# The sums of the output weights' quarters, formed on VectorE behind the first half of the first y instead of on GpSimd

## The chip, the core and the metric

The kernel runs on one core of one Trainium2 chip. Its time is the device time of one execution in microseconds; the time before is 693.48 us, the median of 3 runs (693.12 to 696.33). In the text PE is TensorE's matrix engine, PEld its weight loads, DVE is VectorE, ACT ScalarE, POOL GpSimd, and SP the engine that issues the DMAs.

## The reference, cut to what matters

The program is a chain of three stages on a batch of 4 with 576 positions and 512 channels: an attention (a pooled one and a local one, added), a mixer with two pairs of weights, and a last mixer with cosines and sines. Only the last is touched by the change:

```python
theta = x @ w_theta
zr, zi = x * np.cos(theta), x * np.sin(theta)
y = einsum('ts,bsd->btd', w_tok_r, zr) + einsum('ts,bsd->btd', w_tok_i, zi)
u = x + y
out = u + np.maximum(u @ w_ch, 0.0)
```

All of it is float32 and has to stay so. Each operand of a product is therefore split in two parts that TensorE takes at full rate, a high part and the rest (names that end in h and l), and each product is three matmuls: high by high, high by low, low by high (`mm3`, lines 137 to 139). `split` (lines 132 and 133) makes the parts: a cast on ACT and a subtraction on DVE.

## The kernel before, in words

Attention and the first mixer are issued in an order written out by hand, a table at the head of the kernel. The last mixer, which comes after that table, is written as a loop over the four batches `b`; there the framework's scheduler decides by a timeline of its own in which order the instructions stand on each engine. Within one engine the order is then fixed, and each engine works through its queue in that order, waiting on semaphores of the others.

Per batch the last mixer has four steps.
- `stage_z`: the product th of the transposed x (`xh`, `xl`) with `w_theta`, in blocks of 128 positions. Each block is evicted by ACT (`tt`, line 843), its angle reduced on DVE (`tf`, lines 844 and 847), cosine and sine taken on ACT (`tg` and `tf`, lines 849 to 851), multiplied by x on DVE (line 855; line 863 for the last 64 positions, which two batches share in tiles `eh`, `el`), and split into `zh` and `zl` (lines 132 and 133). For batch 0 it is called twice, for columns 0 to 255 and 256 to 511, with names th_0_... and th_256_...; for the others once.
- `stage_y`: y in four quarters of channels, each in two halves of 288 positions. A quarter's half is 27 matmuls of 288 columns (9 blocks of `z` by three). `stage_y(b, 0, ...)` makes the first two quarters (four results, 108 matmuls), `stage_y(b, 1, ...)` the other two (108 more). Line 879 adds each result to x in place, on DVE.
- sums of u for a scheme with seven products instead of eight (`first_sum`, `other_sums`, `split_sums`, with the tile `us`, which shares a buffer by the tag raw).
- `stage_out`: the seven products of `u` with `w_ch` (banks named o_a to o_d), combined and stored.

The seven products also need sums of the quarters of `w_ch`, once for all batches. That is `weight_sums`: `wc_whole` is the whole of the weights, high plus low, 2048 columns a partition; four sums of 512 columns follow (`wc_sums`), three of which are split into `sums` and `suml` and one into a quarter of `wch` and `wcl`. It is called in batch 0 behind the first `stage_y`, and is done on POOL, except for the two splits. `wc_whole` has no buffer of its own: it takes the one of the tag x in `cells["cx"][1]` that `load_x(1)` will fill with the x of batch 1 (tile cx, a DMA of 1152 KB, line 733). So that load waits for the last reader of `wc_whole`. `load_x(b)` also loads x in the other orientation (cxn, line 739). The x of batch 1 is split into `cxh` and `cxl` (line 1015 of the kernel before, 1017 of the changed one), which th of batch 1 needs.

Of the kernel before, what the change touches and what calls it, by code (L numbers as in the profile page):

```python
# [12 lines left out]
F32 = mybir.dt.float32  # L13
# [6 lines left out]
ALU = mybir.AluOpType  # L20
# [67 lines left out]
HALF = S // 2  # L88
# [10 lines left out]
def kernel(  # L99
# [16 lines left out]
    act, dve, pool, pe, sp = nc.scalar, nc.vector, nc.gpsimd, nc.tensor, nc.sync  # L116
# [14 lines left out]
    def split(hi, lo, src):  # L131
        act.copy(hi, src)  # L132
        dve.tensor_tensor(out=lo, in0=src, in1=hi.bitcast(F32), op=ALU.subtract)  # L133

    def mm3(out, lh, ll, rh, rl, start, stop, again=False):

        pe.matmul(out, lh, rh, start=start, stop=False, skip_group_check=again)  # L137
        pe.matmul(out, lh, rl, start=False, stop=False, skip_group_check=again)  # L138
        pe.matmul(out, ll, rh, start=False, stop=stop, skip_group_check=again)  # L139
# [589 lines left out]
    def load_x(b):  # L729

        x = cells["cx"][b % 2].tile([128, 4, S if b % 2 else 640], F32, tag="x", name=f"cx_{b}")
        src = xT_d.rearrange("(k p) n -> p k n", p=128)
        sp.dma_start(x[:, :, 0:S], src[:, :, b * S : b * S + S])
        if b % 2 == 0:

            sp.dma_start(x[:, :, S:640], src[:, :, b * S + S + 512 : b * S + 2 * S])
        xn = cells["cx"][0].tile([128, NB, DM], F32, tag="xn", name=f"cxn_{b}", bufs=1)
        rows = xN_d[b * S : b * S + S]
        sp.dma_start(xn[:, 0:4], rows[0:512].rearrange("(k p) d -> p k d", p=128))
        if b % 2 == 0:  # L740
            for j in range(2):
                sp.dma_start(xn[64 * j : 64 * j + 64, 4], xN_d[(b + j) * S + 512 : (b + j) * S + S])
        return x, xn

    def split_x(b, x):
        xh = cells["cs"].tile([128, 4, 640], F32R, tag="xh", name=f"cxh_{b}")
        xl = cells["cs"].tile([128, 4, 640], F32R, tag="xl", name=f"cxl_{b}")
        n = 512 if b % 2 else 640
        steps = []
        for kb in range(4):  # L750
            h, l, r = xh[:, kb, 0:n], xl[:, kb, 0:n], x[:, kb, 0:n]
            steps.append(partial(act.copy, h, r))
            steps.append(partial(dve.tensor_tensor, out=l, in0=r, in1=h.bitcast(F32), op=ALU.subtract))
        return (xh, xl), steps
# [55 lines left out]
    op = ctx.enter_context(tc.tile_pool(name="op", bufs=2))  # L810
    turns = count()

    def bank(name):
        return psum(next(turns), name)

    cells["cx"].append(ctx.enter_context(tc.tile_pool(name="cx1", bufs=1, side="right")))
    thh, thl, wrh, wrl, wch, wcl = (cells[name] for name in ("thh", "thl", "wrh", "wrl", "wch", "wcl"))
# [3 lines left out]
    def new_z(b):  # L821
        z = tuple(sb1.tile([128, 8, DM], F32R, tag=f"z{p}", name=f"z{p}_{b}") for p in "hl")
        for e in range(0 if b % 2 else 2):
            last[b + e] = [sb2.tile([128, DM], F32R, tag=f"e{p}", name=f"e{p}_{b + e}") for p in "hl"]
        return z
# [43 lines left out]
    def stage_y(b, hh, x, uh, ul, zh, zl):  # L869
        for db in range(2):  # L870
            k = 2 * hh + db
            c = slice(k * 128, (k + 1) * 128)
            for th in range(2):
                t = slice(th * HALF, (th + 1) * HALF)
                ps = bank(f"y_{b}_{hh}_{db}_{th}")
                for kb in (8, 0, 1, 4, 5, 2, 3, 6, 7):
                    h, l = (e[:, c] for e in last[b]) if kb == 8 else (zh[:, kb, c], zl[:, kb, c])
                    mm3(ps[:, 0:HALF], h, l, wrh[:, kb, t], wrl[:, kb, t], kb == 8, kb == 7)
                dve.tensor_tensor(out=x[:, k, t], in0=ps[:, 0:HALF], in1=x[:, k, t], op=ALU.add)  # L879
            n = S if hh else HALF  # L880
            split(uh[:, k, 0:n], ul[:, k, 0:n], x[:, k, 0:n])

    T0, T1 = slice(0, HALF), slice(HALF, S)
    sums = sb1.tile([128, 3, 2, 256], F32R, name="sums")
# [2 lines left out]
    def raw_sums(name, shape):  # L887
        both = sb1.tile([128, 4 * 2 * HALF], F32, tag="raw", name=name)
        n = 2 * shape
        return [both[:, i * n : (i + 1) * n].rearrange("p (k n) -> p k n", k=2) for i in range(4)], both  # L890

    def weight_sums():

        w = cells["cx"][1].tile([128, 4, S], F32, tag="x", name="wc_whole")[:, :, 0:DM]
        pool.tensor_tensor(out=w, in0=wch.bitcast(F32), in1=wcl.bitcast(F32), op=ALU.add)
        a11, a12, a21, a22 = w[:, 0:2, 0:256], w[:, 2:4, 0:256], w[:, 0:2, 256:DM], w[:, 2:4, 256:DM]
        (s1, s2, s4, s3), both = raw_sums("wc_sums", 256)
        pool.tensor_tensor(out=s1, in0=a21, in1=a22, op=ALU.add)
        pool.tensor_tensor(out=s2, in0=s1, in1=a11, op=ALU.subtract)
        pool.tensor_tensor(out=s4, in0=a12, in1=s2, op=ALU.subtract)  # L900
        pool.tensor_tensor(out=s3, in0=a11, in1=a21, op=ALU.subtract)
        split(*(t.rearrange("p a k n -> p (a k n)") for t in (sums, suml)), both[:, 0 : 3 * 512])
        split(wch[:, 0:2, 256:DM], wcl[:, 0:2, 256:DM], s3)

    def first_sum(b, x):

        (t1, *rest), both = raw_sums(f"us_{b}", HALF)
        dve.tensor_tensor(out=t1, in0=x[:, 0:2, T1], in1=x[:, 0:2, T0], op=ALU.subtract)
        return t1, *rest, both

    def split_sums(b, raws, i, n):
        if i == 0:
            raws += tuple(
                cells["cs"].tile([128, 4, 2, HALF], F32R, tag=tag, name=f"{tag}s_{b}") for tag in ("xh", "xl")
            )
        both, *hl = raws[4:]
        h, l = (t[:, i : i + n].rearrange("p a k n -> p (a k n)") for t in hl)
        split(h, l, both[:, i * 2 * HALF : (i + n) * 2 * HALF])
        return raws

    def other_sums(b, x, raws):

        t1, t2, t3, t4 = raws[0:4]
        dve.tensor_tensor(out=t2, in0=x[:, 2:4, T1], in1=t1, op=ALU.subtract)
        dve.tensor_tensor(out=t3, in0=x[:, 2:4, T1], in1=x[:, 0:2, T1], op=ALU.subtract)
        dve.tensor_tensor(out=t4, in0=x[:, 2:4, T0], in1=t2, op=ALU.subtract)
# [73 lines left out]
    z = new_z(0)  # L1000
    stage_z(0, 0, 256, *xhl, xx[1], *z)
    stage_z(0, 256, DM, *xhl, xx[1], *z)
    for b in range(B):
        x, xn = xx
        uh = sb1.tile([128, 4, S], F32R, tag="uh", name=f"cuh_{b}")
        ul = sb1.tile([128, 4, S], F32R, tag="ul", name=f"cul_{b}")
        stage_y(b, 0, x, uh, ul, *z)
        if b == 0:
            weight_sums()
        raws = first_sum(b, x)  # L1010
        if b + 1 < B:
            xx = load_x(b + 1)
            xhl, steps = split_x(b + 1, xx[0])
            for st in steps:
                st()
        else:
            raws = split_sums(b, raws, 0, 1)
        stage_y(b, 1, x, uh, ul, *z)
        other_sums(b, x, raws)
        if b + 1 < B:  # L1020
            z = new_z(b + 1)
            stage_z(b + 1, 0, DM, *xhl, xx[1], *z)
            raws = split_sums(b, raws, 0, 1)
        split_sums(b, raws, 1, 1)
        split_sums(b, raws, 2, 2)
        stage_out(b, x, uh, ul, *raws[-2:])
# [70 lines left out]
```

## Time and profile before

| | |
|---|---|
| runs of the kernel | 693.12, 693.48, 696.33 us |
| the profiled execution's own time | 693.91 us |
| its span | 692.1 us |
| PE busy | 666.8 us, 96% of the span |
| DVE, ACT, POOL busy | 474.2, 304.4 and 106.6 us |
| share of the chain that ended last: PE, DVE, DMA, ACT | 85%, 5%, 5%, 2% |

The busy times are a first hint only: an engine can be busy with something that nobody waits for. The chain that ended last is followed back from the end, and says at each step what released the next. [...] A row of a timeline is: start in us, duration in us, engine, line, operation, what it writes and reads, shape, count, and in brackets the idle time before it and who ended that. Starts are counted from the start of the span; the hand-ordered part ends at about 472 us, where the last mixer begins.

### The profile page before, as it was taken

What the parts mean: (1) busy time and instruction counts of PE and PEld (TensorE: products, weight loads), DVE (VectorE), ACT (ScalarE), POOL (GpSimd) and SP (SyncE); (2) the same over time, 40 slices, a digit from 0 to 9 for tenths busy, and PEclk for the clock granted to TensorE, in tenths of its full rate; (3) what the DMA queues carried; (4) which work ended last, traced back from release to release, by engine and by line L of the source; (5) the groups of instructions that cost most, each with busy time, mean ns of one, the idle gap of its engine ahead of it and who ended that gap; (6) DMA issues with size and microseconds to landing.
All of it is one profiled execution on the core that took longest, in us unless ns stands there. A gap on an engine that the chain in (4) does not pass through costs nothing.

```text
span 692.1 us, 17284 instructions
## 1 busy us (share of the span) xinstructions
PE 666.8 (96%) x7368; PEld 637.1 (92%) x7368; DVE 474.2 (69%) x835; ACT 304.4 (44%) x594; POOL 106.6 (15%) x84
## 2 busy tenths in 40 slices
PE   7679899999999999999999999999799999999997
PEld 5558789999999999999999999999798998998997
DVE  6798998764543888997783423446967847857837
ACT  4466667352442565656361212113646326526311
POOL 3143222201000332452421000003200000000000
PEclk9779999999999999999999999999999999999999
DMA  8697787554334776744473483465210420140202
GB/s 286 207 283 230 247 279 252 182 175 137 125 107 158 230 241 212 229 156 141 143 203 75 121 228 95 94 159 114 70 62 1 135 87 0 52 147 1 70 1 69
DMA packets 85613, 100.36 MB, mean 145 GB/s; under 512 B 44257, under 2 KB 65889, under 8 KB 85537
## 3 DMA queue, kind: packets, MB, share of 16 engines
q1 hardware_dynamic: 85536, 99.27, 46.6%
q8 instruction: 58, 0.95, 0.6%
q14 instruction: 19, 0.15, 0.1%
HBM read 74.34 MB, written 24.90 MB: 143 GB/s over the span
## 4 chain that ended last, share of the span: by engine, by line
PE 85%; DVE 5%; DMA 5%; ACT 2%; issue 1%; SPq 1%; DVEq 0%; ACTq 0%
PE c L646 7%; PE c L137 7%; PE c L138 7%; PE c L649 7%; PE c L139 7%; PE c L647 7%; PE y L139 6%; PE y L137 6%; PE y L138 6%; PE t L137 2%; PE th L139 2%; PE th L138 2%; PE th L137 2%; PE t L138 2%; PE t L139 2%; PE o L515 1%
## 5 line engine op out<-in xcount | busy, mean ns | idle before, releaser
L190 POOL TENSOR_TENSOR ww<-ww,raw 128x512 int32<-128x512 int32 (+2 forms) x43 | 65.3, 1524 | 186.0 <-DVE ww L186 89.2
L662 ACT ACTIVATE g<-c 128x384 fp32r<-128x384 f32 x72 | 34.3, 493 | 105.8 <-PE c L139 90.5
L137 PE MATMUL y<-wrh,zh 128*128 128x288 f32 x256 | 75.6, 298 | 3.2 <-ACT zh L132 3.2
L138 PE MATMUL y<-wrl,zh 128*128 128x288 f32 x256 | 75.5, 297 | 0.0
L139 PE MATMUL y<-wrh,zl 128*128 128x288 f32 x256 | 73.5, 297 | 0.4 <-DVE zl L133 0.4
L665 DVE SCALAR_TENSOR_TENSOR g<-c,g 128x384 fp32r<-128x384 f32 x72 | 37.8, 551 | 46.3 <-ACT g L662 39.5
L673 DVE TENSOR_TENSOR ut<-c,ut 128x384 f32<-128x384 f32 x48 | 25.7, 549 | 38.1 <-PE c L649 29.2
L137 PEld LDWEIGHTS y<-wrh,zh 128*128 128x128 f32 x256 | 48.5, 190 | 3.5 <-ACT zh L132 3.5
L138 PEld LDWEIGHTS y<-wrl,zh 128*128 128x128 f32 x256 | 48.5, 189 | 0.0
L139 PEld LDWEIGHTS y<-wrh,zl 128*128 128x128 f32 x256 | 47.6, 189 | 0.8 <-DVE zl L133 0.8
L173 ACT ACTIVATE ww<-raw 128x512 f32<-128x512 f32 (+2 forms) x43 | 29.2, 679 | 24.7 <-DMA raw<-w_ch 10.1
L879 DVE TENSOR_TENSOR cx<-y,cx 128x288 f32<-128x288 f32 x32 | 14.6, 456 | 35.7 <-PE y L139 35.3
L132 ACT CAST cuh<-cx 128x288 fp32r<-128x288 f32 (+1 forms) x16 | 8.9, 554 | 61.6 <-DVE cx L879 61.6
L174 ACT ACTIVATE raw<-raw 128x512 int32<-128x512 uint32 (+3 forms) x48 | 31.9, 665 | 0.0
L139 PE MATMUL th<-thh,cxl 128*128 128x512 f32 (+1 forms) x92 | 31.6, 343 | 0.0
L138 PE MATMUL th<-thl,cxh 128*128 128x512 f32 (+1 forms) x92 | 31.6, 343 | 0.0
L137 PE MATMUL th<-thh,cxh 128*128 128x512 f32 (+1 forms) x92 | 31.6, 343 | 0.0
L186 DVE SCALAR_TENSOR_TENSOR ww<-raw,ww 128x512 uint32<-128x512 uint32 (+2 forms) x43 | 30.4, 707 | 1.5
L176 DVE TENSOR_SCALAR ww<-ww 128x512 f32<-128x512 f32 (+2 forms) x43 | 22.9, 532 | 4.8 <-ACT ww L173 4.5
L178 DVE TENSOR_SCALAR ww<-ww 128x512 uint32<-128x512 uint32 (+2 forms) x43 | 23.1, 537 | 1.5
L843 ACT ACTIVATE tt<-th 128x512 f32<-128x512 f32 (+1 forms) x19 | 10.7, 571 | 25.6 <-PE th L139 24.3
L345 POOL TENSOR_TENSOR vd<-vd 128x650 f32<-128x650 f32 x8 | 11.8, 1478 | 63.5 <-DMA vd<-vtok 63.5
(290 smaller groups left out, 2154.5 us busy)
## 6 DMA issues: line engine op xcount, KB each, us to landing
raw<-w_ch SPq DMA_DIRECT2D x28, 512.0 KB
qk<-qkT SPq DMA_DIRECT2D x16, 582.0 KB
xT<-ut SPq DMA_DIRECT2D x12, 768.0 KB
vd<-vtok SPq DMA_DIRECT2D x8, 650.0 KB
raw<-w_ri SPq DMA_DIRECT2D x9, 576.0 KB
vw<-vloc SPq DMA_DIRECT2D x32, 146.2 KB
uT<-us SPq DMA_DIRECT2D x16, 288.0 KB
ut<-uT SPq DMA_DIRECT2D x6, 768.0 KB
```

The costliest lines, as they stand in the source:

```text
L137: pe.matmul(out, lh, rh, start=start, stop=False, skip_group_check=again)
L138: pe.matmul(out, lh, rl, start=False, stop=False, skip_group_check=again)
L139: pe.matmul(out, ll, rh, start=False, stop=stop, skip_group_check=again)
L173: act.activation(w, high, AF.Abs)
L174: act.activation(f, words[:, :, 0], AF.Copy, scale=2.0**-29)
L186: dve.scalar_tensor_tensor(out=wu, in0=words[:, :, 1], scalar=0xC0000000, in1=wu, op0=ALU.bitwise_and, op1=ALU.bitwise_or)
L190: pool.tensor_tensor(out=w.bitcast(I32), in0=w.bitcast(I32), in1=f, op=ALU.add)
L646: pe.matmul(ps[:, 0:MIX], h[:, cb % 2, d], h1, start=cb == cbs[0], stop=False)
L647: pe.matmul(ps[:, 0:MIX], l[:, cb % 2, d], h1, start=False, stop=False)
L649: pe.matmul(ps[:, 0:MIX], weight[cb // 2][2][:, cb % 2, d], h2, start=False, stop=cb == cbs[-1])
L662: act.activation(h1, ps, AF.Relu)
L665: dve.scalar_tensor_tensor(out=h2, in0=ps, scalar=0.0, in1=h1.bitcast(F32), op0=ALU.max, op1=ALU.subtract)
```

## The change

`weight_sums` uses DVE in place of POOL for its five operations, and is issued only after the last addition of the first `stage_y` (the result y_0_1_1: batch 0, second quarter, second half). For that `stage_y` returns its last addition. Nothing is removed.

```diff
@@ stage_y
                 for kb in (8, 0, 1, 4, 5, 2, 3, 6, 7):
                     h, l = (e[:, c] for e in last[b]) if kb == 8 else (zh[:, kb, c], zl[:, kb, c])
                     mm3(ps[:, 0:HALF], h, l, wrh[:, kb, t], wrl[:, kb, t], kb == 8, kb == 7)
-                dve.tensor_tensor(out=x[:, k, t], in0=ps[:, 0:HALF], in1=x[:, k, t], op=ALU.add)
+                added = dve.tensor_tensor(out=x[:, k, t], in0=ps[:, 0:HALF], in1=x[:, k, t], op=ALU.add)
             n = S if hh else HALF
             split(uh[:, k, 0:n], ul[:, k, 0:n], x[:, k, 0:n])
+        return added
@@ weight_sums
-        pool.tensor_tensor(out=w, in0=wch.bitcast(F32), in1=wcl.bitcast(F32), op=ALU.add)
+        dve.tensor_tensor(out=w, in0=wch.bitcast(F32), in1=wcl.bitcast(F32), op=ALU.add)
...
-        pool.tensor_tensor(out=s1, in0=a21, in1=a22, op=ALU.add)
-        pool.tensor_tensor(out=s2, in0=s1, in1=a11, op=ALU.subtract)
-        pool.tensor_tensor(out=s4, in0=a12, in1=s2, op=ALU.subtract)
-        pool.tensor_tensor(out=s3, in0=a11, in1=a21, op=ALU.subtract)
+        dve.tensor_tensor(out=s1, in0=a21, in1=a22, op=ALU.add)
+        dve.tensor_tensor(out=s2, in0=s1, in1=a11, op=ALU.subtract)
+        dve.tensor_tensor(out=s4, in0=a12, in1=s2, op=ALU.subtract)
+        dve.tensor_tensor(out=s3, in0=a11, in1=a21, op=ALU.subtract)
@@ the loop over batches
-        stage_y(b, 0, x, uh, ul, *z)
+        added = stage_y(b, 0, x, uh, ul, *z)
         if b == 0:
-            weight_sums()
+            with tc.issue_after(added.ins):
+                weight_sums()
```

Up to the first products y the order on every engine is the same as before; behind it the scheduler set the instructions anew. In the lists below a row is: line, operation, what it writes and reads with the numbers of the tiles, shape.

On DVE, at the first split of `z` of batch 0, the difference is this (- is before, + is now):

```order
 L855 TENSOR_TENSOR tg_0_0_6600<-tg_0_0_6600,cxn_5950 128x512
 L855 TENSOR_TENSOR tf_0_0_6599<-tf_0_0_6599,cxn_5950 128x512
-L133 TENSOR_TENSOR wcl<-wc_sums,wch 128x2x256
 L133 TENSOR_TENSOR zl_6538<-tg_0_0_6600,zh_6537 128x2x256
 L855 TENSOR_TENSOR tg_0_2_6640<-tg_0_2_6640,cxn_5950 128x512
```

The split of a sum of weights (`wcl`) stood ahead of the first `zl`, and is gone from there.

Where the five sums now stand on DVE, behind the addition of y_0_1_1 (this is the changed kernel alone; before, the second split `suml` stood some 30 rows earlier, ahead of the third `zl`):

```order
L879 TENSOR_TENSOR cx_5947<-y_0_1_1_6854,cx_5947 128x288
L133 TENSOR_TENSOR zl_6538<-tg_256_2_6750,zh_6537 128x2x256
L896 TENSOR_TENSOR wc_whole<-wch,wcl 128x4x512
L133 TENSOR_TENSOR zl_6538<-tf_256_2_6749,zh_6537 128x2x256
L899 TENSOR_TENSOR wc_sums<-wc_whole 128x512
L902 TENSOR_TENSOR wc_sums<-wc_whole 128x512
L900 TENSOR_TENSOR wc_sums<-wc_sums,wc_whole 128x512
L901 TENSOR_TENSOR wc_sums<-wc_whole,wc_sums 128x512
L133 TENSOR_TENSOR wcl<-wc_sums,wch 128x2x256
L879 TENSOR_TENSOR cx_5947<-y_1_0_0_6912,cx_5947 128x288
L879 TENSOR_TENSOR cx_5947<-y_1_0_1_6941,cx_5947 128x288
L133 TENSOR_TENSOR suml<-wc_sums,sums 128x1536
```

The first sum stands ahead of the last `zl` of batch 0, the other four behind it, and the splits `wcl` and `suml` among the additions of the second `stage_y`.

On PE, behind the last matmul of y of batch 0 (y_1_1_1), where th of batch 1 begins (the names th_0_0 to th_0_3 are its four blocks):

```order
 L139 MATMUL y_1_1_1_7001<-wrh,zl_6538 128x288
+L137 MATMUL th_0_0_7037<-thh,cxh_6902 128x512
 L138 MATMUL th_0_0_7037<-thl,cxh_6902 128x512
+L137 MATMUL th_0_1_7065<-thh,cxh_6902 128x512
+L138 MATMUL th_0_1_7065<-thl,cxh_6902 128x512
+L137 MATMUL th_0_2_7093<-thh,cxh_6902 128x512
+L138 MATMUL th_0_2_7093<-thl,cxh_6902 128x512
+L137 MATMUL th_0_3_7121<-thh,cxh_6902 128x512
+L138 MATMUL th_0_3_7121<-thl,cxh_6902 128x512
+L137 MATMUL o_0_a<-cuh_6763,wch 128x288
+L138 MATMUL o_0_a<-cul_6764,wch 128x288
+L139 MATMUL o_0_a<-cuh_6763,wcl 128x288
```

Before, the first matmuls of th_0_0 stood among those of y, and the four blocks came one after the other; now all of th comes behind all of y, two matmuls of each block first, and four of the first output product among them. On SP the load of cxn for batch 1 now stands ahead of that of cx, and not behind it.

## Rows read from the trace of the kernel before

**Rows 1.** Chain that ended last, where the last mixer begins: start us, us, engine, tile, line.

```profile
474.42 3.12 DVE tf L844
...
491.69 0.61 PE y L139
```

**Rows 2.** Waits of PE, 470 to 692 us: in total, times, longest.

```profile
PE y L137 <- ACT zh L132: 3.2, 1, 3.2
PE y L139 <- DVE zl L133: 0.4, 1, 0.4
```

**Rows 3.** Busy us (and instructions) of PE, PEld, DVE, ACT, POOL; clock, DMA share, GB/s.

```profile
491.00:688.00 197.00, 196.53 (x1353) 189.46 (x1351) 140.79 (x265) 84.39 (x149) 0.00 (x0) 0.99 0.17 58
```

**Rows 4.** Timeline of PE, 486 to 540 us: y, th and first products of batch 1.

```profile
486.76 0.29 PE L137 MATMUL y<-wrh,eh 128*128 128x288 f32 x1
...
490.54 0.51 PE L137 MATMUL y<-wrh,zh 128*128 128x288 f32 x1 [3.22 <-ACT zh L132]
...
503.00 0.30 PE L137 MATMUL y<-wrh,eh 128*128 128x288 f32 x1
...
506.61 0.29 PE L137 MATMUL y<-wrh,eh 128*128 128x288 f32 x1
...
521.90 0.39 PE L138 MATMUL th<-thl,cxh 128*128 128x512 f32 x1
...
522.37 0.39 PE L137 MATMUL th<-thh,cxh 128*128 128x512 f32 x1
...
531.90 0.30 PE L137 MATMUL o_a<-cuh,wch 128*128 128x288 f32 x1
...
535.49 0.29 PE L138 MATMUL o_c<-xls,sums 128*128 128x288 f32 x1
```

**Rows 5.** One-microsecond stretches, columns as in the third group.

```profile
490.00:491.00 1.00, 0.46 (x2) 0.40 (x2) 1.00 (x3) 1.00 (x2) 0.00 (x0) 0.84 0.70 78
...
493.00:494.00 1.00, 1.00 (x6) 1.00 (x5) 0.93 (x3) 1.00 (x2) 0.00 (x0) 0.50 0.98 381
...
494.00:495.00 1.00, 1.00 (x9) 1.00 (x8) 1.00 (x2) 1.00 (x3) 0.00 (x0) 0.96 0.12 42
```

**Rows 6.** Durations by line, DVE, 470 to 692 us: ns shortest/median/longest, first and last start.

```profile
L844 DVE TENSOR_SCALAR tf<-tt x19: 295/423/3105, 474.4 to 643.1; 128x512 f32<-128x512 f32 x17, 128x256 f32<-128x256 f32 x2
...
L847 DVE TENSOR_TENSOR tf<-tt,tf x19: 424/686/1776, 477.6 to 645.5; 128x512 f32<-128x512 f32 x17, 128x256 f32<-128x256 f32 x2
...
L855 DVE TENSOR_TENSOR tg<-tg,cxn x16: 679/686/1751, 488.1 to 649.5; 128x512 f32<-128x512 f32 x16
...
L133 DVE TENSOR_TENSOR xls<-us,xhs x12: 750/754/1356, 533.0 to 680.9; 128x576 fp32r<-128x576 f32 x8, 128x1152 fp32r<-128x1152 f32 x4
...
L133 DVE TENSOR_TENSOR el<-tt,eh x6: 417/556/1515, 481.6 to 588.3; 128x256 fp32r<-128x256 f32 x4, 128x512 fp32r<-128x512 f32 x2
...
L133 DVE TENSOR_TENSOR suml<-wc_sums,sums x1: 1751/1751/1751, 494.2 to 494.2; 128x1536 fp32r<-128x1536 f32 x1
```

**Rows 7.** Timeline of POOL, 360 to 560 us: the first sum, and two of four.

```profile
472.76 4.62 POOL L895 TENSOR_TENSOR wc_whole<-wch,wcl 128x2048 f32<-128x2048 f32 x1 [107.58 <-PE c L649]
...
483.44 1.30 POOL L898 TENSOR_TENSOR wc_sums<-wc_whole 128x512 f32<-128x512 f32 x1 [6.06 <-ACT tg L849]
...
487.69 1.60 POOL L900 TENSOR_TENSOR wc_sums<-wc_whole,wc_sums 128x512 f32<-128x512 f32 x1
```

**Rows 8.** Timeline of ACT, 470 to 565 us.

```profile
474.00 0.39 ACT L843 ACTIVATE tt<-th 128x256 f32<-128x256 f32 x1 [17.52 <-PE th L139]
...
489.87 0.62 ACT L132 CAST zh<-tg 128x512 fp32r<-128x512 f32 x1 [0.54 <-DVE tg L855]
...
526.66 0.60 ACT L843 ACTIVATE tt<-th 128x512 f32<-128x512 f32 x1 [2.12 <-PE th L139]
...
560.07 2.61 ACT L1015 CAST cxh<-cx 128x640 fp32r<-128x640 f32 x4 [4.34 <-DMA cx<-xT]
```

**Rows 9.** Timeline of SP's queue: the loads of x for batches 1 and 2.

```profile
489.31 0.38 SPq L733 DMA_DIRECT2D cx<-xT  x1
...
552.61 0.39 SPq L733 DMA_DIRECT2D cx<-xT  x1
```

**Rows 10.** Timeline of DVE, 470 to 565 us.

```profile
483.84 1.18 DVE L844 TENSOR_SCALAR tf<-tt 128x512 f32<-128x512 f32 x1 [0.30 <-ACT tt L843]
...
486.38 1.78 DVE L847 TENSOR_TENSOR tf<-tt,tf 128x512 f32<-128x512 f32 x1
...
491.56 0.68 DVE L855 TENSOR_TENSOR tg<-tg,cxn 128x512 f32<-128x512 f32 x1
492.16 0.68 DVE L855 TENSOR_TENSOR tf<-tf,cxn 128x512 f32<-128x512 f32 x1
...
533.04 0.75 DVE L133 TENSOR_TENSOR xls<-us,xhs 128x576 fp32r<-128x576 f32 x1
```

## Prediction

> **What bounds the kernel now.** I read the chain of waits first. Through the last mixer it is PE from 491.69 us to the end; ahead of that it leaves PE for a chain over ACT and DVE that begins with a DVE instruction of 3.12 us at 474.42 us [rows 1]. Then the waits of PE: from 470 to 692 us PE waits for others twice, 3.2 us for the first zh and 0.4 us for the first zl of batch 0 [rows 2]. From 491 to 688 us it is busy for 196.53 of 197 us [rows 3]. So in this stretch time is bought only where PE stands or runs slowly, and whatever moves PE's work ahead at 491 us reaches the end undiminished, as long as no new wait comes.
>
> What the two waits cost is read from PE's timeline. The first y begins at 486.76 us, and the 108 matmuls of the first half of y are through at 506.61 us, where the second half begins: 19.85 us [rows 4]. The last 27 of them, from 503.00 to 506.61, take 3.61 us, or 0.1337 us each [rows 4]; 108 at that pace are 14.44 us. The stand and what follows it cost 19.85 - 14.44 = 5.41 us: 3.63 us of waiting and 1.78 us in matmuls that run slowly behind it. [...]
>
> Why zh is late: the durations by line and POOL's timeline, side by side. DVE's line 844 takes 0.42 us in the median and 0.295 us at its shortest, on the 256 columns that it also has at 474.42 us, where it takes 3.105 [rows 6]. There POOL is in its sum of 2048 columns, 472.76 to 477.38 us [rows 7], and the DVE instruction ends 0.14 us behind it. The four short sums stand on POOL back to back from 483.44 to 489.29 us [rows 7], and there four DVE instructions in a row are stretched: line 844 takes 1.18 us [rows 10], and el, line 847 and the first of line 855 take 1.515, 1.776 and 1.751 against medians or usual values of 0.42, 0.686 and 0.686 [rows 6]. DVE loses 2.81 + 0.75 + 1.09 + 1.09 + 1.07 = 6.81 us, nearly all of it in the chain from the first eviction (ACT, 474.00) to the first zh (489.87, ending 490.49) [rows 8].
>
> [...]
>
> **The change, part by part.** *POOL's five sums go.* The 6.81 us come out of the chain, so the first zh ends near 490.49 - 6.81 = 483.7 us and its zl some 0.7 us later. PE reaches them only at 486.76 plus three matmuls, 487.16 us: 2.7 us of margin. For the three other pairs of zh and zl that y_0_0_0 needs DVE has five instructions of 512 columns left, 0.60 us from start to start [rows 10], and two of 256 (0.30 and 0.42) for the next block: up to 484.5 + 3.7 = 488.2 us. PE needs the last of them 31 matmuls behind 486.76, at 490.9 us. Both waits go, and with them the slow stretch: -5.41 us. What is late next is PE itself; it has no other work to wait for until 501.2 us (486.76 + 14.44).
>
> *DVE gets five sums.* The trace has none of 2048 columns on DVE. From below, 1536 columns take 1.751 us; from above, POOL took 4.62 [rows 6, 7]. By the slope between 576 and 1536 columns, (1.751 - 0.750) / 960, it is 1.751 + 512 x 0.00104 = 2.28 us, and I take that, being near the lower row. [...] The four of 512 columns stand at 0.69 (line 847's median; bounds 0.42 and POOL's 1.60), back to back 0.60 [rows 10]. They stand behind the addition of y_0_1_1, which waits for PE's 501.2, so 501.4 to 501.85; a zl, 0.6; the big sum to 504.7; the last zl to 505.3; four sums to 507.8 us. Queued behind are that zl and the additions of the second half of y. PE needs the last zl some 52 matmuls behind 501.2 us, at 508.1: 2.8 us of margin. The sums of weights are first needed by products at 517 us, and their splits (1.75 us for suml on DVE, no longer for its cast on ACT) are through by about 512. Cost: nothing, hidden by 14.44 us of y on PE.
>
> *The load of cx for batch 1* waits for those sums. Before, it was issued at 489.31 us, as POOL ended [rows 9], and had landed at about 494.1, where the DMA share falls from 0.98 to 0.12 [rows 5]: 4.8 us. Now it goes at 507.8. Bounds of its flight: 4.8, and 7.46 us for batch 2's load with a second one behind it (552.61 to ACT's cast at 560.07) [rows 8, 9]. With 0.6 us for the first cast (512 columns, as zh's) [rows 8], cxh is there at 513.2 to 515.9 us; nearest is the same transfer, 513.2. PE asks for it at 501.2 + 14.44 = 515.64 us. Between 2.4 us of margin and 0.3 us of wait; I take no wait. SP has cxn ahead of it in its queue, free when DVE has read the old one at about 501 us, so this does not hold it up.
>
> *th of batch 1 in another order.* Its second block, for which ACT's chain waits, is now complete behind 28 th matmuls and 4 products, not 4.76 us after the last y (521.90 to 526.66) [rows 4, 8]. A th matmul takes (531.90 - 522.37) / 42 = 0.227 us [rows 4], so 28 x 0.227 + 4 x 0.134 + 0.2 = 7.1 us: 2.35 us later against the end of y. The first product that uses the chain's xls stood at 535.49, 13.59 us after the last y [rows 4]; now 48 th (4 of which came earlier before) and 27 products lie between, 14.5 us, or 0.94 later. Before, xls was written at 533.79 [rows 10], 1.70 us ahead of PE. Margin now: 1.70 - 2.35 + 0.94 = 0.29 us. Thin; from above it could cost some tenths, from below nothing can be gained. I take 0.
>
> **Sum.** -5.41 us and nothing else. The profiled execution took 693.91 us (span 692.1 us, 1.8 around it), 0.43 above the median of the runs, 693.48. It would take 688.50; against the median, 688.07. Predicted: 688.1 us.
>
> **The rivals.**
> 1. *Part of it is given back at th of batch 1*: by a late cx (landing beyond 515.0 us) or by the thin margin at xls. For it: the load moves 18.5 us back, and batch 2's took 7.46. Against: 2.4 us of margin at the same transfer's own time. A stand of 1 us, and half of the 1.78 for the clock behind it: 688.1 + 1.9 = 690.0.
> 2. *POOL is not what holds DVE up*, and the stretched instructions stay: then only the splits wcl and suml leave the way of the first zl, worth the 0.4 us wait and a little of what follows, some 0.8 us: 692.7. For it: nothing in the trace names a holder. Against: every stretched instruction lies beside a POOL sum, and the same lines are at their median elsewhere.
> 3. *Slower: the sums are as slow on DVE as on POOL.* 4.62 + 5.85 in place of 4.7 us [rows 7] puts their end at 513.6, cx at 518.4 to 521.1, cxh at 519.0 to 521.7. PE would stand 3.4 to 6.1 us at 515.64, and 1.78 for the clock: 5.2 to 7.9 against the gain of 5.41, so 693.3 to 696.0; I put it at 695. It decides where the sums end later than 513.9 us. Against: the row of 1536 columns in 1.751 us.
>
> **How the numbers follow.** 0.5% of the median, about what a measurement of this kernel tells from no change, is 3.5 us: faster is below 690.0. Chances: forecast 0.80, rival 1 0.10, rival 2 0.05, rival 3 0.05. The forecast alone spans 687.3 to 688.9: 0.4 us of scatter to either side (the lower two of the three runs are 0.36 apart) and a few tenths at xls. For 8 in 10 I reach down to 687.1 and through most of rival 1, to 690.9. Faster: the forecast and 0.06 of rival 1, 0.86. Same: 0.04 of rival 1, rival 2 and 0.02 of rival 3, 0.11. Slower: 0.03.
>
> **What would show it.** Right: no wait of PE at 487 us, granted clock 1.00 from 486 to 500 us, line 844 at 0.3 us at 474 us, the second half of y beginning near 501.2, the big sum on DVE at 2.3 us, and PE's waits empty to the end. Wrong: a wait of th of batch 1 for cxh, with the clock at 0.50 behind it (rivals 1 and 3), a wait of o_c for xls (rival 1), or DVE's line 844 still at 3 us with POOL idle (rival 2).

## Result and profile after

The changed kernel takes 688.76 us in the median of five runs (686.19 to 689.01); five runs of the kernel before, on the same chip, gave 696.2 (693.12 to 699.66). The ratio is 0.9892, with a 95% interval from 0.9849 to 0.9935. A second set of six runs gave 688.57 against 695.23 (25 runs of before): 0.9915 (0.9889 to 0.9941). The forecast was 688.1 us, a gain of 5.41 us or a ratio of 0.9922, which lies in both intervals.

The profiled execution of after took 689.01 us, with a span of 687.2 us, 4.9 us less than before. But the first y began 0.53 us later in it. So what the change can move is better measured alone: **span less the start of the first y**. Before, that is 692.1 - 486.76 = 205.34 us [rows 4]; after, 687.2 - 487.29 = 199.91. The gain there is 5.43 us. The second execution (span 686.7, first y at 486.78) gives 199.92.

The timeline of PE after. A row is start in us, duration, engine, line, operation, what it writes and reads:

```profile
487.29 0.29 PE L137 MATMUL y<-wrh,eh 128*128 128x288 f32 x1
...
487.68 0.30 PE L137 MATMUL y<-wrh,zh 128*128 128x288 f32 x1
...
501.69 0.29 PE L137 MATMUL y<-wrh,eh 128*128 128x288 f32 x1
...
516.08 0.39 PE L137 MATMUL th<-thh,cxh 128*128 128x512 f32 x1
...
530.61 0.29 PE L138 MATMUL o_c<-xls,sums 128*128 128x288 f32 x1
```

No row of PE from 470 us to the end has a wait in brackets, and its list of waits there is empty; before, it had 3.2 and 0.4 us [rows 2]. The second half of y begins 501.69 - 487.29 = 14.40 us behind the first matmul (before 19.85; forecast 14.44), and th of batch 1 at 516.08, 14.39 us later. From start to start, a matmul of the split parts with 288 columns takes 0.133 us there (14.40 / 108), or 0.46 ns a column. In the trace of before, bf16 has 0.43 ns (line 280 from 10.80 us, 320 columns in 0.136 us), and transpositions of unsplit float32 have 0.85 (line 505 from 62.64 us, 128 columns in 0.109 us). The clock has no dip; the columns here are the stretch, its length, the busy times of PE, PEld, DVE, ACT and POOL with counts, the granted clock (1.00 is full speed), DMA share and GB/s:

```profile
490.00:491.00 1.00, 1.00 (x9) 1.00 (x9) 0.55 (x2) 0.84 (x2) 0.00 (x0) 1.00 0.00 0
493.00:494.00 1.00, 1.00 (x10) 1.00 (x9) 0.96 (x2) 0.50 (x2) 0.00 (x0) 1.00 0.00 0
```

Those two stretches stood at 0.84 and 0.50 before [rows 5]; in the second, PE had 6 matmuls then and has 10 now. The cause is to be read in DVE's timeline, where the same instructions have their short durations, and the five sums follow behind y_0_1_1:

```profile
474.95 0.30 DVE L844 TENSOR_SCALAR tf<-tt 128x256 f32<-128x256 f32 x1 [0.68 <-ACT tt L843]
...
481.90 0.42 DVE L133 TENSOR_TENSOR el<-tt,eh 128x256 fp32r<-128x256 f32 x1
482.24 0.69 DVE L847 TENSOR_TENSOR tf<-tt,tf 128x512 f32<-128x512 f32 x1
482.84 0.69 DVE L855 TENSOR_TENSOR tg<-tg,cxn 128x512 f32<-128x512 f32 x1
...
502.86 2.28 DVE L896 TENSOR_TENSOR wc_whole<-wch,wcl 128x2048 f32<-128x2048 f32 x1
...
507.58 0.69 DVE L901 TENSOR_TENSOR wc_sums<-wc_whole,wc_sums 128x512 f32<-128x512 f32 x1
...
529.59 0.75 DVE L133 TENSOR_TENSOR xls<-us,xhs 128x576 fp32r<-128x576 f32 x1
```

Line 844 takes 0.30 us (3.10 before), el 0.42 (1.515), line 847 0.69 (1.776), line 855 0.69 (1.751) [rows 6]. The large sum takes 2.28 us, as worked out from the slope of two other widths, and the sums end at 507.58 + 0.69 = 508.27 us. ACT and SP after:

```profile
483.65 0.61 ACT L132 CAST zh<-tg 128x512 fp32r<-128x512 f32 x1
...
514.97 2.18 ACT L1017 CAST cxh<-cx 128x512 fp32r<-128x512 f32 x4 [3.92 <-DMA cx<-xT]
...
523.22 0.60 ACT L843 ACTIVATE tt<-th 128x512 f32<-128x512 f32 x1 [1.22 <-PE th L139]
```

```profile
508.36 0.36 SPq L733 DMA_DIRECT2D cx<-xT  x1
```

The first zh ends at 483.65 + 0.61 = 484.26 us; PE reaches it at 487.68, with 3.4 us to spare, where it was 3.2 us late. The cast of cxh begins only 6.61 us behind the load.

### The profile page after: what moved, and what is told of

The parts are those of the page before. It is cut to its first block, busy times and chain, and to the rows that moved or that the text cites. A ratio compares the mean times of both kernels' runs of the same rounds, so it can differ in the third digit from the quotient of the medians.

```text
span 687.2 us, 17270 instructions
## 1 busy us (share of the span) xinstructions
PE 663.0 (96%) x7368; PEld 634.5 (92%) x7368; DVE 472.0 (69%) x840; ACT 304.8 (44%) x594; POOL 96.8 (14%) x79
## 4 chain that ended last, share of the span: by engine, by line
PE 87%; DMA 5%; DVE 5%; ACT 1%; issue 1%; SPq 0%; POOL 0%; DVEq 0%; POOLq 0%; ACTq 0%
PE c L646 7%; PE c L138 7%; PE c L137 7%; PE c L649 7%; PE c L647 7%; PE c L139 7%; PE y L137 6%; PE y L138 6%; PE y L139 6%; PE th L138 2%; PE th L137 2%; PE th L139 2%; PE t L137 2%; PE t L138 2%; PE t L139 2%; PE o L515 1%
## 5 line engine op out<-in xcount | busy, mean ns | idle before, releaser
L515 PE MATMUL o<-vw,plt 38*32 38x65 f32 x1280 | 17.9, 236 | 6.7 <-DVE pbuf L493 4.8
L515 PEld LDWEIGHTS o<-vw,plt 38*32 38x32 f32 x1280 | 15.3, 110 | 9.4 <-DVE pbuf L493 5.0
```

What stands on the lines that cost most here:

```text
L515: pe.matmul(o[r : r + 32, 5 * j + i // 2], pts[h : h + W, i // 2, r : r + 32], vw[h : h + W, g, :], start=True, stop=True,)
```

## The experiments

Each is compared by its runs, and by span less first y in its one profile; the latter is far sharper. In twelve profiles the first y started anywhere between 485.30 and 491.79 us, while span less first y agrees to 0.11 us among the five profiles in which PE does not wait behind the first y (199.91 to 200.02). The last two columns are from the profile. The runs' medians also hold the scatter ahead of the first y, which the change does not touch.

| kernel | median us | ratio to before (95%) | span less first y | waits of PE behind the first y |
|---|---|---|---|---|
| before | 693.09 to 696.2 | 1 | 205.34 | 3.2 zh, 0.4 zl |
| after | 688.76 | 0.9892 (0.9849 to 0.9935) | 199.91 | none |
| again | 688.57 | 0.9915 (0.9889 to 0.9941) | 199.92 | none |
| pool_extra | 693.88 | 0.9989 (0.9967 to 1.001) | 205.60 | 3.0 zh, 0.2 zl |
| pool_fill | 690.14 | 0.9938 (0.9912 to 0.9963) | 199.96 | none |
| pool_copy | 690.78 | 0.9921 (0.9879 to 0.9964) | 199.92 | none |
| pool_big | 688.06 | 0.9921 (0.9888 to 0.9954) | 200.40 | none listed; 0.3 and 0.1 by its starts |
| pool_four | 691.3 | 0.9941 (0.9916 to 0.9967) | 201.71 | 1.3 zl |
| dve_early | 689.53 | 0.9922 (0.9895 to 0.995) | 200.02 | none |
| pool_late | 695.3 | 0.9989 (0.9966 to 1.0012) | 205.35 | 3.4 zh |
| pool_tied | 695.87 | 1.0022 (0.9994 to 1.005) | 207.01 | 4.0 cxh |
| dve_twice | 692.99 | 0.9976 (0.9952 to 1.0001) | 202.11 | 1.9 cxh |

**again.** The changed kernel once more.

> The changed kernel once more, beside the three that follow. Every theory expects what its first five runs gave, 686.2 to 689.0 us, and in its profile no wait of PE from 470 us on. It settles how much of the 0.5 us by which the work ahead of the first y came later is scatter: the first y stood at 486.76 us before the change and at 487.29 behind it, with the same order of instructions up to there.

Its first y stood at 486.78 us, so the 0.53 us were scatter of the part ahead, which this change does not touch.

**pool_extra.** The question is whether POOL's sums, or the new order, made PE wait. `extra` repeats all five operations of `weight_sums` on POOL, in scratch tiles.

```diff
+    def extra():
+        w = cells["cx"][1].tile([128, 4, S], F32, tag="x", name="ex_whole")[:, :, 0:DM]
+        pool.tensor_tensor(out=w, in0=wch.bitcast(F32), in1=wcl.bitcast(F32), op=ALU.add)
+        (s1, s2, s4, s3), both = raw_sums("ex_sums", 256)
+        a11, a12, a21, a22 = w[:, 0:2, 0:256], w[:, 2:4, 0:256], w[:, 0:2, 256:DM], w[:, 2:4, 256:DM]
+        pool.tensor_tensor(out=s1, in0=a21, in1=a22, op=ALU.add)
...
         if b == 0:
+            extra()
             with tc.issue_after(added.ins):
                 weight_sums()
```

> The changed kernel, with five POOL sums of the same kind added at their old place (their results go to scratch tiles that nobody reads; the sums in use stay on DVE, late). All other engines have the changed kernel's order word for word. Theory 1 (a POOL sum that reads SBUF stops DVE for as long as it runs): the stretched DVE instructions are back, 6.8 us in all (line 844 at 3.1 us at 475 us), the first zh is 6.8 us later than the 484.26 us of the changed kernel, 491.0, PE waits 3.4 us for it at 487.68 and runs some 1.8 us slower behind it: 688.8 + 5.2 = 694.0 us. Theory 2 (the gain came from the new order and from the splits that no longer stand ahead of the first zl): no wait, 688.8 us, within 0.5.

Measured: 693.88 us, and in the profile the waits of PE are back:

```profile
PE y L137 <- ACT zh L132: 3.0, 1, 3.0
PE y L139 <- DVE zl L133: 0.2, 1, 0.2
```

Its POOL and its DVE side by side:

```profile
473.69 4.62 POOL L896 TENSOR_TENSOR ex_whole<-wch,wcl 128x2048 f32<-128x2048 f32 x1 [107.44 <-DMA xN<-turned]
483.05 1.70 POOL L899 TENSOR_TENSOR ex_sums<-ex_whole 128x512 f32<-128x512 f32 x1 [4.74 <-DVE el L133]
```

```profile
475.36 3.10 DVE L844 TENSOR_SCALAR tf<-tt 128x256 f32<-128x256 f32 x1 [0.68 <-ACT tt L843]
...
483.63 1.41 DVE L863 TENSOR_TENSOR tt<-tg,cxn 64x256 f32<-64x256 f32 x1
485.05 1.42 DVE L863 TENSOR_TENSOR tt<-tf,cxn 64x256 f32<-64x256 f32 x1
486.57 1.33 DVE L844 TENSOR_SCALAR tf<-tt 128x512 f32<-128x512 f32 x1
487.82 1.49 DVE L133 TENSOR_TENSOR el<-tt,eh 128x256 fp32r<-128x256 f32 x1
```

Line 844 again ends (478.46) 0.15 us behind POOL's sum (478.31). Beside the four short sums other lines are hit than before, but by as much: 1.41, 1.42, 1.33 and 1.49 us in place of 0.42, 0.42, 0.43 and 0.43 make 3.95 us, with the 2.81 of line 844 6.76 (6.81 before). The order on PE, DVE, ACT and SP is that of the changed kernel, splits included. So POOL's sums alone cost 205.60 - 199.92 = 5.68 us, 3.2 of them as waits and the rest in matmuls behind them, and the new order brought nothing: rival 2 is out.

**pool_fill.** The same place with POOL instructions that only write, against pool_extra.

```diff
-        pool.tensor_tensor(out=w, in0=wch.bitcast(F32), in1=wcl.bitcast(F32), op=ALU.add)
+        for _ in range(2):
+            pool.memset(w, 1.0)
-        pool.tensor_tensor(out=s1, in0=a21, in1=a22, op=ALU.add)
...
+        for t in (s1, s2, s4, s3, s1, s2, s4, s3):
+            pool.memset(t, 1.0)
```

> The changed kernel, with POOL memsets at the old place of the sums: two of 2048 columns and eight of 512, into scratch tiles that nobody reads. They write as many columns as the sums twice over and read none. Theory 1, in the form that only POOL's reads of SBUF stop DVE: DVE's durations as in the changed kernel (line 844 at 0.3 us), no wait of PE, 688.8 us within 0.5. Theory 1 in the wider form (whatever POOL does in SBUF stops DVE): line 844 as long as the memset beside it, and a wait of PE of 1 to 4 us with slow matmuls behind it, 690.5 to 694.5. Theory 2 (order): 688.8.

POOL's timeline with its memsets and the durations of the two long ones (ns: shortest, median, longest; first and last start), and behind it DVE's beside them:

```profile
473.61 3.73 POOL L897 MEMSET ex_whole<- 128x2048 f32 x2 [107.56 <-DMA xN<-turned]
482.78 3.81 POOL L900 MEMSET ex_sums<- 128x512 f32 x8 [5.44 <-DVE el L133]
L897 POOL MEMSET ex_whole<- x2: 1805/1834/1864, 473.6 to 475.5; 128x2048 f32 x2
```

```profile
475.30 0.30 DVE L844 TENSOR_SCALAR tf<-tt 128x256 f32<-128x256 f32 x1 [0.68 <-ACT tt L843]
...
482.59 0.69 DVE L847 TENSOR_TENSOR tf<-tt,tf 128x512 f32<-128x512 f32 x1
```

Line 847 and the six DVE instructions behind it, all with two inputs, keep their 0.68 to 0.69 us beside the short memsets, and PE waits for nothing. Line 844 takes its 0.30 us too, but that settles less. The first long memset ends at 473.61 + 1.81 = 475.42 and the second begins at 475.47, so line 844 (475.30 to 475.60) lies across the seam between them. Where POOL's sum held it up it ended 0.15 us behind POOL; here that would have been 475.57, within its own 0.30 us. Whether a memset holds line 844 up, no run shows. The median is 1.6 us above that of again, but span less first y is the same (199.96), so the difference is to be looked for ahead of the first y.

**pool_copy.** POOL copies, which read one input, against pool_extra.

```diff
-        pool.tensor_tensor(out=w, in0=wch.bitcast(F32), in1=wcl.bitcast(F32), op=ALU.add)
+        pool.tensor_copy(out=w, in_=wch.bitcast(F32))
-        pool.tensor_tensor(out=s1, in0=a21, in1=a22, op=ALU.add)
...
+        for t in (s1, s2, s4, s3):
+            pool.tensor_copy(out=t, in_=w[:, 0:2, 0:256])
```

> The changed kernel, with POOL copies at the old place of the sums: one of 2048 columns and four of 512, each reading one input in SBUF and writing scratch tiles. It asks whether one input that POOL reads is enough. If reading alone decides: line 844 at 475 us lasts to the end of the copy, and other DVE instructions beside the short copies are stretched to their length; how long a copy takes on POOL no run shows, between the memset's 1.9 us for 2048 columns and the sum's 4.62, so DVE loses 1 to 6 us and PE waits 0 to 3, 688.8 to 694. If it takes two inputs: line 844 at 0.3 us, no wait, 688.8 within 0.5.

POOL's timeline with its copies and the durations of the four short ones (as above), and DVE's beside them:

```profile
475.57 1.89 POOL L896 COPY ex_whole<-wch 128x2048 f32<-128x2048 f32 x1 [107.59 <-DMA xN<-turned]
485.04 3.77 POOL L899 COPY ex_sums<-ex_whole 128x512 f32<-128x512 f32 x4 [7.58 <-ACT tg L850]
L899 POOL COPY ex_sums<-ex_whole x4: 718/1071/1071, 485.0 to 487.7; 128x512 f32<-128x512 f32 x4
```

```profile
477.24 0.37 DVE L844 TENSOR_SCALAR tf<-tt 128x256 f32<-128x256 f32 x1 [0.68 <-ACT tt L843]
...
485.20 1.10 DVE L855 TENSOR_TENSOR tg<-tg,cxn 128x512 f32<-128x512 f32 x1
```

One input that POOL reads is enough: four DVE instructions in a row take 1.09 to 1.10 us in place of 0.68, and start 1.02 us apart; those behind them are at 0.68 again. The copies are longer in turn: the first takes 0.72 us, the other three 1.07, and they too start 1.02 us apart. The large copy was nearly through as line 844 came, and cost it 0.08. In all DVE loses 1.7 us, less than the slack of 3.4, and PE waits for nothing.

**pool_big and pool_four.** Parts of pool_extra: `extra` with the large sum alone, and with the four short ones alone, read from quarters of `wch`, since there is no whole.

```diff
+        pool.tensor_tensor(out=w, in0=wch.bitcast(F32), in1=wcl.bitcast(F32), op=ALU.add)
```

```diff
+        v = wch.bitcast(F32)
+        a11, a12, a21, a22 = v[:, 0:2, 0:256], v[:, 2:4, 0:256], v[:, 0:2, 256:DM], v[:, 2:4, 256:DM]
+        pool.tensor_tensor(out=s1, in0=a21, in1=a22, op=ALU.add)
+        pool.tensor_tensor(out=s2, in0=s1, in1=a11, op=ALU.subtract)
+        pool.tensor_tensor(out=s4, in0=a12, in1=s2, op=ALU.subtract)
+        pool.tensor_tensor(out=s3, in0=a11, in1=a21, op=ALU.subtract)
```

> The changed kernel, with only the 2048-column sum added on POOL at its old place (into a scratch tile). Theory 1 with slack: one DVE instruction is stretched, by 2.8 us, the first zh ends near 484.26 + 2.8 = 487.1 us, which is 0.6 us ahead of PE's 487.68; no wait, 688.8 us within 0.5. If instead each stretched microsecond costs its share (2.8 of 6.8 of the whole 5.4): 688.8 + 2.2 = 691.0. Theory 2 (order): 688.8.

In pool_big, the stretched instruction in DVE's timeline, and two matmuls that follow each other in PE's:

```profile
472.96 3.10 DVE L844 TENSOR_SCALAR tf<-tt 128x256 f32<-128x256 f32 x1 [0.68 <-ACT tt L843]
```

```profile
486.37 0.29 PE L139 MATMUL y<-wrh,zl 128*128 128x288 f32 x1
486.79 0.40 PE L137 MATMUL y<-wrh,zh 128*128 128x288 f32 x1
```

> The changed kernel, with only the four 512-column sums added on POOL (into scratch tiles, in the order of the old ones). Theory 1 with slack: four DVE instructions in a row are stretched, by 4.0 us in all. The first zh keeps some tenths to one us of its 3.4 us of slack, and the zl behind it come about when PE wants them: PE waits 0 to 1 us in all, 688.8 to 690.3 us. With the 2048-column sum alone costing nothing and both costing 5.4 us or so, the two together would then cost more than their sum. If each stretched microsecond costs its share (4.0 of 6.8 of 5.4): 692.0. Theory 2 (order): 688.8.

In pool_four, the first and the last of four stretched instructions in DVE's timeline, and PE's list of waits:

```profile
481.34 1.79 DVE L855 TENSOR_TENSOR tg<-tg,cxn 128x512 f32<-128x512 f32 x1
...
486.46 1.77 DVE L855 TENSOR_TENSOR tg<-tg,cxn 128x512 f32<-128x512 f32 x1
```

```profile
PE y L139 <- DVE zl L133: 1.3, 1, 1.3
```

The large sum alone stretches line 844 to 3.10 us as before, and costs 0.48 us of span less first y, not a share of the whole (2.2). That is not quite the nothing that was expected: the first zh comes in time, but PE starts 486.79 - 486.37 = 0.42 us apart where 0.13 is its pace, since the second zh (ACT, 486.12 + 0.61 = 486.73) has less slack. The four alone stretch four instructions to 1.77 to 1.79 us and cost 1.79 us, more than the wait of 0 to 1 us that was expected; 1.3 of them are a wait for zl. Separately they cost 0.48 + 1.79 = 2.27 us, together 5.68: a stall was paid only where it exceeded the slack, and only the longer wait of pool_extra has matmuls at a clock of 0.50 behind it (494 to 496 us). pool_four's granted clock stays at 1.00 through its 1.3 us of wait.

**dve_early.** The engine without the place.

```diff
         if b == 0:
-            with tc.issue_after(added.ins):
-                weight_sums()
+            weight_sums()
```

> The engine of the changed kernel without its place: the five sums on DVE, where the scheduler puts them when nothing holds them back (the first ahead of the last transposition, the others and their splits among the first zl). Theory 1: no stretched instruction, but 2.3 us and then 4 x 0.6, 0.6 and 1.75 us stand in DVE's queue ahead of the zl that PE wants, against 3.4 us of slack and 2.3 us in which DVE idles there: PE waits 0 to 2 us, 688.8 to 692. So the engine alone brings more than half of the gain. If the place brought the gain: 693 to 695.

DVE's timeline, with the large sum and the instruction behind it that POOL had stretched:

```profile
476.47 2.28 DVE L896 TENSOR_TENSOR wc_whole<-wch,wcl 128x2048 f32<-128x2048 f32 x1
...
479.16 0.25 DVE L844 TENSOR_SCALAR tf<-tt 128x256 f32<-128x256 f32 x1
```

The sums stand on DVE where POOL had them in time, nothing is stretched, and nothing waits: 200.02 us, 689.53 in the median. The engine alone brings the whole gain. The place behind y_0_1_1 adds nothing that these runs show.

**pool_late.** This was to be the place without the engine: all five sums on POOL again, with the tie.

```diff
-        dve.tensor_tensor(out=w, in0=wch.bitcast(F32), in1=wcl.bitcast(F32), op=ALU.add)
+        pool.tensor_tensor(out=w, in0=wch.bitcast(F32), in1=wcl.bitcast(F32), op=ALU.add)
...
```

> The place of the changed kernel without its engine: the five sums stand behind the addition of y_0_1_1, but on POOL. Theory 1: the 0.5 us windows ahead of the first y are as in the changed kernel (no wait there), so the whole gain up to the second half of y is there; the sums last to about 502.4 + 4.6 + 4 x 1.5 = 513 us, the load of cx for batch 1 goes out there and its cast begins 6.6 us later, at 519.6, so that cxh is late against PE's 516.1 us by about 4 us, with slow matmuls behind it: 688.8 + 4 to 6, 693 to 695 us (rival 3's price). If the engine were all and the place nothing: as slow as before for another reason, with PE's wait at 487 us again.

POOL's timeline and PE's list of waits:

```profile
477.24 4.62 POOL L896 TENSOR_TENSOR wc_whole<-wch,wcl 128x2048 f32<-128x2048 f32 x1 [107.60 <-DMA xN<-turned]
```

```profile
PE y L137 <- ACT zh L132: 3.4, 1, 3.4
```

It did not test that. The tie sets the order in which the program issues instructions, but made no engine wait here. POOL had nothing else in its queue, so its first sum still ran 14 us ahead of the first y (491.25), and span less first y is that of before to 0.01 us. On DVE the tie works, because the addition and the sums share a queue: in after they start at 501.88 and 502.86 us.

**pool_tied.** The same with a true dependency, against pool_late.

```diff
+        pool.tensor_copy(out=w[:, 0, 0:1], in_=x[:, 1, HALF : HALF + 1])
         pool.tensor_tensor(out=w, in0=wch.bitcast(F32), in1=wcl.bitcast(F32), op=ALU.add)
```

> The five sums on POOL, and truly late: a POOL copy of one column of the result y_0_1_1 stands ahead of them and makes POOL wait for it (the first sum then overwrites that column). Measure: span less the start of the first y, 199.9 us in the changed kernel, 205.3 before. Theory 1: no stretched instruction at 475 to 487 us and no wait at the first y; then sums from 502.4 to 513.0 us, the load of cx there, its cast 6.6 us later, the first block of cxh at 520.2 against PE's 516.1: PE waits 4.1 us at th of batch 1 and runs 0 to 1.8 us slower behind it, 204.0 to 205.9, a time of 693 to 695 us (rival 3's price: the place without the engine gives all of it back). By the flight of 4.8 us that the prediction took, the wait is 2.3 us and the measure 202.2 to 204.0.

POOL's timeline (the copy that waits, the last sum), PE's at the new wait, and a stretch behind it:

```profile
504.66 0.42 POOL L896 COPY wc_whole<-cx 128x1 f32<-128x1 f32 x1 [136.85 <-DVE cx L879]
...
514.59 1.62 POOL L902 TENSOR_TENSOR wc_sums<-wc_whole,wc_sums 128x512 f32<-128x512 f32 x1
```

```profile
522.35 0.80 PE L137 MATMUL th<-thh,cxh 128*128 128x512 f32 x1 [4.00 <-ACT cxh L1018]
```

```profile
522.00:528.00 6.00, 5.65 (x17) 4.88 (x18) 3.63 (x6) 2.25 (x5) 0.00 (x0) 0.50 0.00 0
```

Now the wait at the first y is gone, and a new one of 4.0 us stands at th of batch 1, where cxh is late because the load of cx waits for sums that end at 516.21 us. PE's clock is at 0.50 from 522 to 528 us, and the two cost 207.01 - 199.91 = 7.1 us. That is rival 3's wait, here by sums on POOL, and its price lies in the range that it was given (5.2 to 7.9 us): the wait of 4.0 us in 3.4 to 6.1, but the slow matmuls at 3.1 us, where the prediction had taken 1.78 over from y. It makes 1.67 us more than before in this stretch, though the runs (1.0022, 0.9994 to 1.005) do not separate it from before.

**dve_twice.** How near the changed kernel is to that wait.

```diff
-        dve.tensor_tensor(out=w, in0=wch.bitcast(F32), in1=wcl.bitcast(F32), op=ALU.add)
+        for _ in range(2):
+            dve.tensor_tensor(out=w, in0=wch.bitcast(F32), in1=wcl.bitcast(F32), op=ALU.add)
```

> The changed kernel with the 2048-column sum formed twice on DVE (the second writes the same result again), so that the sums end 2.2 us later, at 510.5 us, and the load of cx goes out then. The scheduler also puts 16 more products into the middle of th of batch 1; the first eight matmuls behind y still need cxh. With the flight as the changed kernel shows it (6.6 us to the cast, 0.55 for it): cxh at 517.7 against PE's 516.1, a wait of 1.6 us, span less first y 201.5 to 202.5 (changed kernel 199.9), 690 to 691.5 us. With the flight of 4.8 us and the rule of the prediction that a wait begins only where the sums end later than 513.9 us: no wait, 199.9, 688.8.

DVE's timeline (the second large sum, the last short one) and PE's at th of batch 1:

```profile
510.17 2.28 DVE L897 TENSOR_TENSOR wc_whole<-wch,wcl 128x2048 f32<-128x2048 f32 x1
...
515.79 0.69 DVE L902 TENSOR_TENSOR wc_sums<-wc_whole,wc_sums 128x512 f32<-128x512 f32 x1
```

```profile
522.63 0.50 PE L137 MATMUL th<-thh,cxh 128*128 128x512 f32 x1 [1.88 <-ACT cxh L1018]
```

One more sum, with what the scheduler then moved ahead of the short sums, ends them 515.79 + 0.69 - 491.79 = 24.69 us behind the first y (after: 20.98), and PE waits 1.9 us. The expectation took the prediction's 513.9 us for the point where a wait begins. In the prediction it is the point from which rival 3 eats the whole gain (513.9 + 4.8 + 0.6 - 515.64 = 3.66 us of wait, and 1.78 for the clock). A wait begins, by its flight of 4.8 us and 0.6 for the cast, where the sums end later than 515.64 - 0.6 - 4.8 = 510.2 us, or 23.5 behind the first y. By that PE would have waited some 1.2 us here. So the run shows the 4.8 us as too short, not a wait where none was due: the cast began 5.40 us behind the load, as the cast ahead of it on ACT ended. Span less first y is 2.2 us above that of the changed kernel. The runs say more, 0.6% or some 4 us (0.9976 against 0.9915); the profile places the rest ahead of the first y (491.79), and no run says why.

## Why the prediction was right, point by point

- *POOL's sums hold DVE up, and PE waits for it: -5.41 us.* Right, 5.43 in the profiles. Shown by pool_extra: the sums put back, with nothing else moved, cost 5.68. In these runs it depends on what POOL's instruction reads: beside memsets, which only write, seven DVE instructions with two inputs kept their 0.68 to 0.69 us; beside copies, which read one input, four took 1.09 to 1.10. For line 844, which has one input, the memsets leave it open. Beside sums, the length goes by POOL's instruction and not by DVE's: where POOL's sums take 1.3 to 1.7 us, in pool_extra and pool_four, DVE instructions of 0.42 and of 0.69 us alike last about as long as the sum beside them (1.33 to 1.79). Line 844 shows it best: in pool_extra and in pool_copy it starts 1.67 us into POOL's large instruction and ends 0.15 us behind it, and so takes 3.10 us beside a sum of 4.62 and 0.37 beside a copy of 1.89. So the stretch is no single factor: in before it is 10.5 beside the large sum and 2.6 to 3.6 beside the short ones [rows 6, 10]. By what mechanism POOL holds DVE up, no run shows.
- *2.28 us for the large sum, sums ended at 507.8.* Right: 2.28, and 508.27 with the 0.53 us of the later start, 0.06 off.
- *The load of cx: 4.8 us taken.* This term was mis-sized. It is 6.61 us from the load to ACT's cast in after, 6.75 in again, and 5.44 to 6.75 over all runs in which ACT waited for it. The margin at th is 516.08 - 514.97 - 0.67 (from cast to matmul, as in pool_tied) = 0.44 us, not 2.4; that no wait came is in part luck. The step that failed is the reading of the landing from the DMA share. It falls 4.8 us behind the load in after too (508.36 to 513.2), but then goes on thinly at 0.06, the part of one engine in 16, and the cast follows 0.44 us behind the last packet (514.53):

```profile
512.80:513.00 0.20, 0.20 (x3) 0.20 (x3) 0.20 (x1) 0.00 (x0) 0.00 (x0) 1.00 0.91 355
513.80:514.00 0.20, 0.20 (x4) 0.20 (x3) 0.00 (x0) 0.00 (x0) 0.00 (x0) 1.00 0.06 23
...
514.60:514.80 0.20, 0.20 (x4) 0.20 (x3) 0.00 (x0) 0.00 (x0) 0.00 (x0) 1.00 0.00 0
```

The columns are those of the stretches above; the last is GB/s. In before, where the 4.8 us were read, the share goes on in the same way, to 494.7 us or 5.4 behind the load:

```profile
494.40:494.60 0.20, 0.20 (x4) 0.20 (x2) 0.20 (x1) 0.20 (x2) 0.00 (x0) 1.00 0.06 23
```

The bounds, 4.8 to 7.46, held the flight, so the time is right; the points built on 4.8 are not. A wait begins by after's flight where the sums end near 20.98 + 0.44 = 21.4 us behind the first y, and by the shortest flight, 5.44, 1.2 us later, in place of 23.5. The changed kernel has only some tenths to spare. Rival 3's 513.9 us is too late as well: in pool_tied the sums end 516.21 - 489.39 = 26.82 us behind the first y, 513.6 on before's clock, and cost 7.1 us, more than the whole gain.
- *th of batch 1 in another order, 0.29 us of margin at xls.* Right. The second block was evicted at 523.22, 7.14 us behind y (forecast 7.1); xls was written at 529.59 + 0.75 = 530.34 and taken at 530.61, 0.27 us later.
- *0.4 us of scatter to either side.* Too small. It was taken from the lower two of three runs; eleven runs of after cover 686.19 to 689.93, those of before 691.19 to 699.99. The profiles put it ahead of the first y (485.30 to 491.79). It left the forecast standing, but not without luck. Before's median came out at 696.2 and 695.23 us in the two sets, not at the 693.48 that the forecast started from; with the two ratios 693.48 would have become 686.0 and 687.6, one below the stated range of 687.1 to 690.9. And the time of one run, or the median of three, says less than the term of 5.4 us that was forecast.

## What to carry to other kernels

Before putting work on an idle GpSimd, look for what VectorE does in the same microseconds: here an instruction of 0.30 us took 3.10 beside a GpSimd sum of 4.62, and ended 0.15 us behind it, and instructions of 0.42 and of 0.69 us took 1.33 to 1.79 beside short sums, while seven kept their 0.68 to 0.69 beside memsets, which only write. Such a stall cost only what exceeded the slack of the next engine, so its parts measured one by one did not add up: 0.48 and 1.79 us alone, 5.68 together (pool_big, pool_four, pool_extra). To move work later on another engine, give it a true dependency: with an order of issue alone POOL's first sum began 14 us ahead of the first y (pool_late), with a dependency 16 us behind it (pool_tied). And read a transfer's landing from who waits for it, or where nobody waits from the stretch in which the share reaches 0.00, not from where it falls: in after it fell 4.8 us behind the load, and the reader began at 6.61.

## What was not expected of the hardware

A wait of PE did not always bring the clock down. The stretches right behind the waits of 1.3 us in pool_four and of 1.9 us in dve_twice:

```profile
490.00:491.00 1.00, 1.00 (x10) 1.00 (x9) 1.00 (x3) 0.26 (x1) 0.00 (x0) 1.00 0.00 0
```

```profile
523.00:524.00 1.00, 1.00 (x6) 0.82 (x5) 1.00 (x3) 1.00 (x3) 0.00 (x0) 1.00 0.00 0
```

They stand at 1.00. After the waits of 3.0 us in pool_extra, 3.2 in before and 4.0 in pool_tied the clock fell to 0.50, for some 3 us in pool_extra and before, and for over 6 us in pool_tied, where the matmuls behind the wait were those of th and the first products. Why it stayed low longer there is open.

Open too is why the same 1152 KB took 5.44 to 6.75 us to their first reader, but two traces give a hint. In after the load's last packet ended 6.17 us behind its issue (514.53), and a 16 KB packet of the instruction queue (q8) started 1.19 us behind the issue. In before it ended 5.40 us behind its issue (494.71), with no packet of q8 beside it. In pool_tied the DMA share reached 0.00 within 5.0 us (521.2 against 516.24). That the packet of q8 holds up the engine that ends last is not shown.
